# Decode attention with a cached K and V: 4 MB loads in one ring of five slots, another order of the last loads, wo per group, two K^T buffers, and a V lag of two steps

## The chip, the cores and the metric

The kernel runs on one core of a Trainium2 chip. The core has five engines with instruction streams of their own: TensorE (PE in the profile) for matrix products, VectorE (DVE), ScalarE (ACT), GpSimd (POOL) and SyncE (SP). Sixteen DMA engines move data between the chip's main memory and the core's on-chip memory of 128 partitions; SP and ScalarE start such transfers, each through a queue of its own. Engines wait for each other and for transfers through semaphores, and every engine works through its stream in order.

The metric is the device time of one execution in microseconds, as the median of several runs. One further execution is recorded by the hardware profiler.

## The reference

One token attends to a cache of 65,536 positions. There are 8 groups of K and V, and 2 query heads for each. The result is mixed with a small token MLP through a gate. Cut to what matters:

```python
Hq, Hkv, Sk, Dh = 16, 8, 65536, 256          # D = 448, everything bf16
q = (x @ wq).reshape(B, Sq, Hq, Dh).transpose(0, 2, 1, 3)     # Sq = 1
k = repeat(k_cache, 2, axis=1); v = repeat(v_cache, 2, axis=1)
scores = einsum("bhqd,bhkd->bhqk", q, k) * Dh ** -0.5
o = einsum("bhqk,bhkd->bhqd", softmax(scores), v)
a = o.transpose(0, 2, 1, 3).reshape(B, Sq, Hq * Dh) @ wo

h = layernorm(x)                              # the token MLP
u = gelu(einsum("bsd,sf->bdf", h, w1) + b1)   # F = 1792
b = (einsum("bdf,fs->bds", u, w2) + b2).transpose(0, 2, 1)

g = sigmoid((x * gate_w).sum(-1, keepdims=True))
return g * a + (1 - g) * b
```

K and V are 8 x 65,536 x 256 numbers of 2 bytes each: 268 MB for K and as much for V. Every byte is read once.

## The kernel before

**Tiling.** A chunk is `CH` = 2048 positions of one group: 16 tiles of 128 positions (`NT` = 16). A group has `NCPH` = 32 chunks, the whole kernel `NC` = 256. Position p*16+n of a chunk lies on partition p, so that a load reads one contiguous row of memory for each partition. A load (`DC` = 2) brings two chunks of K or of V: 2 MB, 16 KB on each partition. There are `NCD` = 128 loads of K and 128 of V.

**Loads.** SP issues all large transfers in one order: K load 0, wq in two parts, and then, for each cd, K load cd and V load cd-1 (L203 to L214). K has two buffers (`KB`), V three (`VB`). A K load waits until the transposes of the K load two before it are done (L187, `sem_tr`); a V load waits until the values of the V load three before it are done (L194, `sem_pv`). The last V load goes out in four pieces of 512 KB, each with a semaphore of its own (L199). wo, 3.5 MB, is one load after K load 3 (L213). ScalarE's queue brings the small rows at the start.

**TensorE's steps.** The loop at L327 runs `NC + LAG` steps. Step s does, in this order: the transposes of chunk s (L245: 32 of 128x128, into the four PSUM banks `kst`), the scores of chunk s-1 (L261: 32 products with two columns, from the transposed K in `ktT`), the denominators of chunk s-2 (L272: one product of a matrix of ones with the weights), and the values of chunk s-`LAG` (L287: 32 products with two columns). With `LAG` = 3 the values of a chunk come one step after its denominators. Step 1 also holds the Q projection (L339, L341), which needs wq. The MLP's output products (L308) lie in steps 6 to 19. At a group's end follows the projection with wo (L300, `project`).

**The other engines.** VectorE copies the banks 0 and 2 of each chunk from PSUM into `ktT` (L470), ScalarE the banks 1 and 3 (L533). `ktT` has three buffers (`KTB`); a copy into one waits for the scores that read it last. ScalarE turns scores into weights `pT` (L524, five buffers, `PTB`). VectorE computes the MLP's tiles in the loop's steps 3 to 18 (`b_partA`, `b_partB`), ScalarE their tanh (L518).

**The end.** After the last values VectorE sums the denominators (L450), inverts them (L454) and scales (L447); TensorE multiplies with wo (L300); VectorE adds the row (L461); SP stores it (L216).

Of the kernel before, what the change touches and what calls it, by code (L numbers as in the profile page):

```python
# [11 lines left out]
def bass_gated_mix__gqa_block_cached__mixer_token_mlp__decode_kernel(  # L12
# [25 lines left out]
    P = 128  # L38
# [6 lines left out]
    DC = 2  # L45
    KB = 2
    VB = 3
# [4 lines left out]
    KTB = 3  # L52
    PTB = 5
    LAG = 3
    assert T % (CH * DC) == 0 and NCD > max(KB, VB)

# [7 lines left out]
    PN = 8  # L64
    NPIECE = DC * NT // PN

# [16 lines left out]
    with ctx:  # L83
# [8 lines left out]

        kbuf = sb([P, KB, DC * NT, DH], bf16, "kbuf")
        vbuf = sb([P, VB, DC * NT, DH], bf16, "vbuf")
# [5 lines left out]
        wq_a = sb([P, WF, NQ], bf16, "wq_a")  # L100
        wq_b = sb([P, HALF], bf16, "wq_b")
        wo_sb = sb([P, HQ, 2, DM], bf16, "wo_sb")
# [7 lines left out]
        w1row_b = sb([1, F], bf16, "w1row_b")  # L110
        b1row_b = sb([1, F], bf16, "b1row_b")
        w2row_b = sb([1, F], bf16, "w2row_b")
# [5 lines left out]
        scr_row = sb([1, DM], f32, "scr_row")  # L118
        prod_b = sb([1, DM], bf16, "prod_b")
# [7 lines left out]
        wring = sb([P, NUR, DM], bf16, "wring")  # L127
        tring = sb([P, NUR, DM], bf16, "tring")
        gu = sb([P, NUR, DM], bf16, "gu")
        brow1 = sb([1, DM], bf16, "brow1")  # L130
        brow = sb([1, DM], bf16, "brow")
        run = sb([1, DM], f32, "run")
        out_b = sb([1, DM], bf16, "out_b")

# [3 lines left out]

        sem_k = [new_sem("semk%d" % i) for i in range(KB)]
        sem_v = [new_sem("semv%d" % i) for i in range(VB)]  # L140
        sem_vp = [new_sem("semvp%d" % i) for i in range(NPIECE)]
# [3 lines left out]
        sem_wo = new_sem("sem_wo")  # L145
# [30 lines left out]

        def cache_src(cache, cd, n0=0, n1=DC * NT):
            g, k = divmod(cd * DC, NCPH)
            src = cache[0, g, k * CH:(k + DC) * CH, :].rearrange("(p n) d -> p n d", p=P)
            return src[:, n0:n1, :].rearrange("p n d -> p (n d)")  # L180

        @block.sync
        def _(eng):
            def k_dma(cd):
                slot = cd % KB
                if cd >= KB:
                    eng.wait_ge(sem_tr, NB * (cd - KB + 1) * DC)  # L187
                eng.dma_start(kbuf[:, slot].rearrange("p n d -> p (n d)"), cache_src(A_k_cache, cd)
                              ).then_inc(sem_k[slot], 16)

            def v_dma(cd):
                slot = cd % VB
                if cd >= VB:
                    eng.wait_ge(sem_pv, (cd - VB + 1) * DC)  # L194
                if cd < NCD - 1:
                    eng.dma_start(vbuf[:, slot].rearrange("p n d -> p (n d)"), cache_src(A_v_cache, cd)
                                  ).then_inc(sem_v[slot], 16)
                    return
                for j in range(NPIECE):  # L199
                    eng.dma_start(vbuf[:, slot, j * PN:(j + 1) * PN, :].rearrange("p n d -> p (n d)"),  # L200
                                  cache_src(A_v_cache, cd, j * PN, (j + 1) * PN)).then_inc(sem_vp[j], 16)

            k_dma(0)  # L203
            eng.dma_start(wq_a[:, :, :].rearrange("p j n -> p (j n)"),
                          A_wq[0:WF * P, :].rearrange("(p j) n -> p (j n)", p=P)).then_inc(sem_wq, 16)
            eng.dma_start(wq_b[:, :], A_wq[WF * P:DM, :].rearrange("r (a n) -> (r a) n", a=2)
                          ).then_inc(sem_wq, 16)
            for cd in range(1, NCD + 1):
                if cd < NCD:
                    k_dma(cd)  # L210
                v_dma(cd - 1)
                if cd == KB + 1:
                    eng.dma_start(wo_sb[:, :, :, :].rearrange("p h j n -> p h (j n)"),  # L213
                                  A_wo.rearrange("(h p j) n -> p h (j n)", h=HQ, j=2)).then_inc(sem_wo, 16)  # L214
            eng.wait_ge(s_run, H + 1)
            eng.dma_start(out_row_ap, out_b[:, :]).then_inc(sem_out, 16)  # L216
            eng.wait_ge(sem_out, 16)
# [13 lines left out]
        def _(pe):  # L231
            one = ones_sq[0:1, 0:1]

            def transposes(c):
                cd, ck = divmod(c, DC)
                slot = cd % KB
                if ck == 0:
                    pe.wait_ge(sem_k[slot], 16 * (cd // KB + 1))
                for b in range(NB):
# [3 lines left out]
                    for j in range(8):  # L243
                        ntl, dh = divmod(j, 2)
                        ins = pe.transpose(kst[:, b, j * P:(j + 1) * P],  # L245
                                           kbuf[:, slot, ck * NT + 4 * b + ntl, dh * P:(dh + 1) * P],
# [28 lines left out]
            def values(c):  # L275
                g, k = divmod(c, NCPH)
                cd, cv = divmod(c, DC)
                slot = cd % VB
                if cd < NCD - 1 and cv == 0:
                    pe.wait_ge(sem_v[slot], 16 * (cd // VB + 1))  # L280
                for nt in range(NT):
                    n = cv * NT + nt
                    if cd == NCD - 1 and n % PN == 0:
                        pe.wait_ge(sem_vp[n // PN], 16)
                    for dj in range(2):
                        col = POC + dj * REP
                        ins = pe.matmul(acc[:, g % 2, col:col + REP],  # L287
                                        vbuf[:, slot, n, dj:DH:2],
# [5 lines left out]
            def project(g):  # L294
                pe.wait_ge(s_oTn, g + 1)
                if g == 0:
                    pe.wait_ge(sem_wo, 16)
                for hh in range(REP):
                    for dj in range(2):
                        ins = pe.matmul(acc[0:1, g % 2, PRC:PRC + DM],  # L300
                                        oTn[:, g % 2, dj * REP + hh:dj * REP + hh + 1],
                                        wo_sb[:, g * REP + hh, dj, :],
# [59 lines left out]
        def _(vec):  # L362
# [49 lines left out]
            def b_partA(kt):  # L412
                slot = kt % NUR
                U = uring[:, slot, :]; W = wring[:, slot, :]; Z = zring[:, slot, :]
                if kt >= NUR:
                    vec.wait_ge(s_tanh, kt - NUR + 1)
                    vec.drain()
# [148 lines left out]
```

The softmax here doesn't subtract the row's maximum and nothing guards it: scores larger than these inputs give would overflow.

## Time and profile before

| | |
|---|---|
| median of 4 runs | 1321.25 us (1320.61 to 1322.43) |
| the profiled execution, its own time | 1321.69 us |
| the profiled execution's span, first to last instruction | 1319.9 us |
| TensorE matmuls, busy | 1122.2 us, 85% of the span, 25054 matmuls |
| TensorE weight loads, busy | 1096.7 us, 83% |
| ScalarE, VectorE busy | 546.5 us (41%), 412.8 us (31%) |
| TensorE's clock granted, mean | 0.776 of full speed |
| read from main memory | 544.22 MB, 412 GB/s over the span |
| K loads, issue to landing, median | 12.6 us for 2048 KB |
| V loads, issue to landing, median | 17.3 us for 2048 KB |

The span is what the profile covers; the execution's own time has some 1.8 us more around it. "Busy" is the time in which an instruction of the engine runs; a matmul and the load of the next weights overlap. The weights' load belongs to each matmul here, because K, its transposed form and V are the stationary operands. "Granted clock" is the share of full speed at which the chip ran TensorE's array, which changes between half and full in the records. A wait in the profile names the instruction or transfer that released it; "issue" is time in which an engine waited for nothing that the profile shows. The DMA row of the page is the busy share of the 16 DMA engines.

### The profile page before, as it was taken

The numbers are of one execution on the slowest core, as the hardware profiler recorded it, in microseconds if no ns is written. First come the engines' busy times: TensorE is split into PE (matmuls) and PEld (weight loads), VectorE is DVE, ScalarE is ACT, GpSimd is POOL, SyncE is SP. The second block draws the span as 40 slices with busy tenths as digits, with TensorE's granted clock in tenths as the row PEclk, the third lists the DMA queues.
The fourth block names the chain that finished last, engine by engine and source line by source line (L and its number), as shares of the span: only waits on it lengthen the run. The fifth ranks groups of instructions, "written<-read, shape, count | busy, mean of one in ns | idle before, by whom it ended". The sixth has DMA issues, their size and how long they took to land.

```text
span 1319.9 us, 53238 instructions
## 1 busy us (share of the span) xinstructions
PE 1122.2 (85%) x25054; PEld 1096.7 (83%) x25054; DVE 412.8 (31%) x716; ACT 546.5 (41%) x786; POOL 0.9 (0%) x7
## 2 busy tenths in 40 slices
PE   6689888888899888988888898888878888888888
PEld 5688888888889888888888898888878888788887
DVE  3685223222222222222222222222223222232222
ACT  3344444444434344444433444344433443443343
POOL 0000000000000000000000000000000000000000
PEclk8778777878767787777767877777778777787877
DMA  9999999999999999999999999999999999999996
GB/s 396 422 425 423 419 424 410 425 420 418 426 398 426 425 417 423 423 422 413 411 421 400 424 417 423 423 419 421 414 419 426 411 426 414 412 428 420 422 423 274
DMA packets 39880, 547.64 MB, mean 415 GB/s; under 512 B 4200, under 2 KB 6251, under 8 KB 6894
## 3 DMA queue, kind: packets, MB, share of 16 engines
q1 hardware_dynamic: 39650, 544.23, 98.4%
q8 instruction: 197, 3.23, 1.0%
q14 instruction: 21, 0.17, 0.0%
q10 hardware_dynamic: 12, 0.01, 0.0%
HBM read 544.22 MB, written 0.00 MB: 412 GB/s over the span
## 4 chain that ended last, share of the span: by engine, by line
DMA 52%; PE 45%; issue 2%; DVE 0%; ACT 0%; ACTq 0%; DVEq 0%
DMA kbuf<-in_A_k_cache_dram 51%; PE kst L245 32%; PE acc L287 6%; PE sps L261 6%; DMA b_b<-in_B_b_dram 1%; PE acc L300 1%; PE acc L272 0%; PE sps L339 0%; PE acc L308 0%; ACT L511 0%; PE sps L341 0%; DVE out_b L461 0%; DVE ktT L470 0%; DVE stat L390 0%; ACTq L503 0%
## 5 line engine op out<-in xcount | busy, mean ns | idle before, releaser
L533 ACT ACTIVATE ktT<-kst 128x1024 bf16<-128x1024 bf16 x512 | 512.1, 1023 | 732.0 <-PE kst L245 731.8
L245 PE MATMUL kst<-ident,kbuf 128*128 128x128 bf16 x8192 | 698.1, 263 | 132.7 <-DMA kbuf<-in_A_k_cache_dram 122.5
L245 PEld LDWEIGHTS kst<-ident,kbuf 128*128 128x128 bf16 x8192 | 646.3, 121 | 149.1 <-DMA kbuf<-in_A_k_cache_dram 130.5
L470 DVE COPY ktT<-kst 128x1024 bf16<-128x1024 bf16 x512 | 352.8, 691 | 871.9 <-PE kst L245 858.0
L287 PE MATMUL acc<-pT,vbuf 128*128 128x2 bf16 x8192 | 247.4, 163 | 28.7 <-issue 28.7
L261 PE MATMUL sps<-qT,ktT 128*128 128x2 bf16 x8192 | 252.1, 164 | 19.1 <-issue 18.7
L261 PEld LDWEIGHTS sps<-qT,ktT 128*128 128x128 bf16 x8192 | 246.5, 99 | 20.9 <-issue 20.4
L287 PEld LDWEIGHTS acc<-pT,vbuf 128*128 128x128 bf16 x8192 | 228.7, 98 | 32.1 <-issue 32.1
L524 ACT ACTIVATE pT<-sps 128x32 bf16<-128x32 f32 x256 | 50.2, 196 | 21.1 <-PE sps L261 21.1
L272 PE MATMUL acc<-pT,ones_sq 128*128 128x32 bf16 x256 | 45.7, 179 | 1.0 <-ACT pT L524 0.5
L272 PEld LDWEIGHTS acc<-pT,ones_sq 128*128 128x128 bf16 x256 | 25.0, 98 | 0.0
L300 PE MATMUL acc<-wo_sb,oTn 128*1 128x448 bf16 x32 | 11.2, 484 | 0.9 <-DVE oTn L447 0.8
L323 PE MATMUL acc<-ones_sq,w1row_b 1*128 1x1 bf16 x14 | 0.5, 161 | 10.5 <-DMA b_b<-in_B_b_dram 10.5
L323 PEld LDWEIGHTS acc<-ones_sq,w1row_b 1*128 1x128 bf16 x14 | 0.4, 100 | 10.6 <-DMA b_b<-in_B_b_dram 10.6
L518 ACT ACTIVATE tring<-zring 128x448 bf16<-128x448 bf16 x14 | 8.1, 582 | 0.0
L300 PEld LDWEIGHTS acc<-wo_sb,oTn 128*1 128x1 bf16 x32 | 2.4, 94 | 4.4 <-issue 2.8
L428 DVE TENSOR_TENSOR zring<-uring,wring 128x448 bf16<-128x448 bf16 x14 | 5.5, 392 | 1.4 <-issue 0.4
L422 DVE TENSOR_TENSOR wring<-uring 128x448 bf16<-128x448 bf16 x14 | 5.5, 392 | 1.0
L424 DVE TENSOR_TENSOR zring<-wring,uring 128x448 bf16<-128x448 bf16 x14 | 5.5, 392 | 1.0
L441 DVE TENSOR_TENSOR gu<-wring,tring 128x448 bf16<-128x448 bf16 x14 | 5.5, 392 | 1.0
L308 PE MATMUL acc<-gu,w2p_b 128*1 128x448 bf16 x14 | 5.1, 363 | 0.0
L420 DVE TENSOR_SCALAR uring<-wring,params 128x448 bf16<-128x448 bf16 x14 | 4.7, 336 | 1.1
(68 smaller groups left out, 60.0 us busy)
## 6 DMA issues: line engine op xcount, KB each, us to landing
kbuf<-in_A_k_cache_dram SPq DMA_DIRECT2D x128, 2048.0 KB, 12.6
vbuf<-in_A_v_cache_dram SPq DMA_DIRECT2D x127, 2048.0 KB, 17.3
wo_sb<-in_A_wo_dram SPq DMA_DIRECT2D x1, 3584.0 KB, 23.5
wq_a<-in_A_wq_dram SPq DMA_DIRECT2D x1, 3072.0 KB, 14.7
vbuf<-in_A_v_cache_dram SPq DMA_DIRECT2D x4, 512.0 KB, 12.2
wq_b<-in_A_wq_dram SPq DMA_DIRECT2D x1, 512.0 KB, 15.4
xrow_b<-in_A_x_dram ACTq DMA_DIRECT2D x1, 0.9 KB
grow_b<-in_gate_w_dram ACTq DMA_DIRECT2D x1, 0.9 KB
```

What stands on the lines that cost most here:

```text
L245: ins = pe.transpose(kst[:, b, j * P:(j + 1) * P], kbuf[:, slot, ck * NT + 4 * b + ntl, dh * P:(dh + 1) * P], ident[:, :])
L261: ins = pe.matmul(sps[:, c % 2, 2 * nt:2 * nt + 2], ktT[:, slot, b, j * P:(j + 1) * P], qT[:, dh, REP * g:REP * g + REP], start=(dh == 0), ...
L272: pe.matmul(acc[:, g % 2, DENC:DENC + 2 * NT], ones_sq[:, :], pT[:, c % PTB, :], start=(k == 0), stop=(k == NCPH - 1))
L287: ins = pe.matmul(acc[:, g % 2, col:col + REP], vbuf[:, slot, n, dj:DH:2], pT[:, c % PTB, 2 * nt:2 * nt + 2], start=False, stop=(k == NCPH ...
L300: ins = pe.matmul(acc[0:1, g % 2, PRC:PRC + DM], oTn[:, g % 2, dj * REP + hh:dj * REP + hh + 1], wo_sb[:, g * REP + hh, dj, :], start=(hh ...
L422: vec.tensor_tensor(W, U, U, op=ALU.mult)
L424: vec.tensor_tensor(Z, W, U, op=ALU.mult)
L428: vec.tensor_tensor(Z, U, W, op=ALU.add)
L470: vec.tensor_copy(ktT[:, c % KTB, b, :], kst[:, b, :]).then_inc(sem_evd, 1)
L518: act.activation(tring[:, slot, :], zring[:, slot, :], AF.Tanh).then_inc(s_tanh, 1)
L524: act.activation(pT[:, c % PTB, :], sps[:, c % 2, 0:2 * NT], AF.Exp, scale=scale).then_inc(sem_exp, 1)
L533: act.activation(ktT[:, c % KTB, b, :], kst[:, b, :], AF.Copy).then_inc(sem_eva, 1)
```

## The change

- A load has four chunks: 4 MB, 32 KB on each partition (`DC` = 4), so that there are 64 loads of K and 64 of V.
- K and V share one ring of five slots (`NS`), used in the order of the loads: K0, V0, K1, V1, ... In this list the last K load changes places with the V load before it, so that the end reads K62, K63, V62, V63. Load i waits for the last reader of load i-5: transposes where that was K, values where it was V.
- wq and the MLP's row w2 lie in the ring's last slot at the start, w1 and b1 in the second K^T buffer. Load 4, the first in that slot, waits for the Q projection (`s_q`).
- The last V load goes out in pieces of 32, 16, 8 and 8 tiles (2 MB, 1 MB, 512 KB, 512 KB).
- wo comes in 8 loads of 448 KB, one for each group, into two buffers; load g waits for the projection of group g-2.
- `KTB` goes from 3 to 2, `PTB` from 5 to 4, `LAG` from 3 to 2.
- In the MLP the work row W is one buffer instead of three, tanh writes into its own input, a wait for tanh is dropped and two drains are added for each tile. Several rows of one partition share memory with others that are no longer needed.

```diff
-    DC = 2
-    KB = 2
-    VB = 3
+    DC = 4
+    NS = 5
...
-    KTB = 3
-    PTB = 5
-    LAG = 3
+    KTB = 2
+    PTB = 4
+    LAG = 2
...
+    loads = [(w, cd) for cd in range(NCD) for w in "kv"]
+    loads[-3], loads[-2] = loads[-2], loads[-3]
+    place = {ld: i for i, ld in enumerate(loads)}
...
+    pieces = [(0, 32), (32, 48), (48, 56), (56, 64)]
...
-        kbuf = sb([P, KB, DC * NT, DH], bf16, "kbuf")
-        vbuf = sb([P, VB, DC * NT, DH], bf16, "vbuf")
+        ring = sb([P, NS, DC * NT, DH], bf16, "ring")
...
+        early = ring[:, NS - 1, :, :].rearrange("p n d -> p (n d)")
+        wq_a = early[:, 0:WF * NQ].rearrange("p (j n) -> p j n", j=WF)
+        wq_b = early[:, WF * NQ:WF * NQ + HALF]
...
+        def slot_of(w, cd):
+            i = place[w, cd]
+            return i % NS, 16 * (i // NS + 1)
...
+            def load(i):
+                w, cd = loads[i]
+                slot = i % NS
+                if i == NS - 1:
+                    eng.wait_ge(s_q, 1)
+                if i >= NS:
+                    w0, cd0 = loads[i - NS]
+                    if w0 == "k":
+                        eng.wait_ge(sem_tr, NB * DC * (cd0 + 1))
+                    else:
+                        eng.wait_ge(sem_pv, DC * (cd0 + 1))
+                if i < len(loads) - 1:
+                    eng.dma_start(ring[:, slot].rearrange("p n d -> p (n d)"), cache_src(w, cd)
+                                  ).then_inc(sem_in[slot], 16)
                     return
...
+            def wo_dma(g):
+                if g >= 2:
+                    eng.wait_ge(s_proj, g - 1)
+                eng.dma_start(wo_sb[:, g % 2, :, :],
+                              A_wo[g * REP * DH:(g + 1) * REP * DH, :].rearrange("(h p j) n -> p h (j n)", h=REP, j=2)
+                              ).then_inc(sem_wo[g % 2], 16)
...
+            for i in range(1, len(loads)):
+                load(i)
+                g, r = divmod(i, 2 * NCPH // DC)
+                if r == NCPH // DC:
+                    wo_dma(g)
...
             def b_partA(kt):
                 slot = kt % NUR
-                U = uring[:, slot, :]; W = wring[:, slot, :]; Z = zring[:, slot, :]
-                if kt >= NUR:
-                    vec.wait_ge(s_tanh, kt - NUR + 1)
-                    vec.drain()
+                U = uring[:, slot, :]; W = wtmp[:, :]; Z = zring[:, slot, :]
+                vec.drain()
...
-                U = uring[:, slot, :]; W = wring[:, slot, :]; TT = tring[:, slot, :]
+                U = uring[:, slot, :]; W = wtmp[:, :]; TT = zring[:, slot, :]
                 vec.wait_ge(s_tanh, kt + 1)
+                vec.drain()
```

## The prediction

> **What bounds the kernel now.** I read the page's queue part first, then the waits, then the chain of waits, then the end of the timeline. First the DMA engines: share of 16 engines' span by queue, and busy tenths over 40 slices.
>
> ```profile
> DMA  9999999999999999999999999999999999999996
> ...
> q1 hardware_dynamic: 39650, 544.23, 98.4%
> q8 instruction: 197, 3.23, 1.0%
> ```
>
> The 16 engines are busy from slice 1 to 39, 98.4% of it with K, V and weights. Bytes cannot fall, so only their cost per byte, the head and the tail can move. Next who waits (total us, times, longest us):
>
> ```profile
> SPq L188 <- PE kst L245: 1165.5, 126, 17.3
> ...
> PE kst L245 <- DMA kbuf<-in_A_k_cache_dram: 122.5, 83, 8.4
> ...
> PE acc L287 <- issue: 28.7, 30, 2.2
> ...
> PE sps L261 <- issue: 18.7, 16, 2.4
> ...
> PE kst L245 <- issue: 9.8, 10, 2.7
> ```
>
> SP waits 1165.5 us for the transposes that free a K buffer, yet the engines stay full: when K load 127 is issued at 1289.73, load 126 has 2.8 us to go and a V load of about 5 us stands behind it, 7.8 us of queue. TensorE waits 122.5 us for K and 57.2 us for "issue". TensorE is thus second, by a small margin. How fast it can go, from the timeline (start, us, ...):
>
> ```profile
> 635.98 1.96 PE L245 MATMUL kst<-ident,kbuf 128*128 128x128 bf16 x32 [0.54 <-DMA kbuf<-in_A_k_cache_dram]
> ...
> 639.41 1.95 PE L245 MATMUL kst<-ident,kbuf 128*128 128x128 bf16 x32
> ...
> 645.76 3.59 PE L245 MATMUL kst<-ident,kbuf 128*128 128x128 bf16 x32 [2.80 <-DMA kbuf<-in_A_k_cache_dram]
> ...
> 650.93 3.57 PE L245 MATMUL kst<-ident,kbuf 128*128 128x128 bf16 x32
> ```
>
> A step (transposes, scores, denominators, values) is 639.41-635.98 = 3.43 us at full clock and 650.93-645.76 = 5.17 us at half clock; after a wait of 2.8 us the clock is half. DMA brings a step's 2 MB in 5.1 us. Last the end, from the chain of waits:
>
> ```profile
> 1289.73 12.51 DMA kbuf<-in_A_k_cache_dram
> ...
> 1302.29 2.80 PE kst L245 x32
> ...
> 1306.80 3.40 PE kst L245 x32
> 1310.20 0.78 PE sps L261 x32
> ...
> 1313.47 1.70 PE acc L287 x64
> ...
> 1315.91 1.67 PE acc L300 x4
> ...
> 1317.67 0.67 DVE out_b L461
> ```
>
> The last K lands at 1302.25, the last V piece at 1312.07 (its semaphore's record), so 4 MB took 9.8 us; TensorE ends its values at 1315.17. From last landing to the span's end: 1319.9-1312.1 = 7.8 us.
>
> **The change, part by part.** The trace keeps a record of every DMA packet (start, time, size; part 3 sums them). Median times: 4 bytes (semaphore) 0.009 us, 1792 bytes 0.074, 4 KB 0.159, 16 KB 0.611, 24 KB (wq_a) 0.912. These lie on one line: 0.009 us each plus 0.0367 us per KB. K and V now go as 16 KB rows, 8 per engine and load.
>
> *4 MB loads.* Rows of 32 KB would take 0.009+1.204 = 1.213 us against 2 x 0.611 = 1.222. Per engine 2072 K and V packets become 1048: 1024 x 0.009 = 9.2 us less. Of 262 DMAs on SP 142 remain; 120 semaphore packets per engine x 0.009 = 1.1 us less. Bounds: 1.1 us if the 9 ns is not per row, 10.3 if it is. I take 10.3; 24 KB, the nearest row, lies on the line. The 16 KB mean is 0.624, not 0.611, 26.6 us per engine in all; the long packets come in bursts on several engines at once, so I keep that per byte (if per packet, 13 us less: the lower end). The last landing moves to 1312.1-10.3 = 1301.8.
>
> [...]
>
> *Ring of five 32 KB slots.* K load c waits for the values of V load c-3, V load c for the transposes of K load c-2: 20 MB where 10 MB were buffered, so two to three loads of 9.9 us are queued. SP is in order: behind each wait stands the next load alone, which is wanted two loads later. DMA cannot run dry in steady state. The head: load 4 holds wq and waits for the Q projection (20.6 us in the trace, some 5 us later now, because K load 0 is twice as long and the small ACT loads, landed by 13.1 now, take turns with packets twice as long); loads 0 to 3 and wq keep DMA busy to 1.7+4x9.9+8.6 = 50 us, which covers it. If not covered it would cost its lateness once.
>
> *wo per group.* Same 2048 packets of 1792 bytes, 7 more DMAs of about 0.4 us on SP, which waits most of the time; each is asked for half a group before its use and its wait on an old projection is long past. Nothing.
>
> *Two K^T buffers, PTB 4, shared work rows, two more drains per mixer tile.* The eviction of chunk c needs the scores of c-2, which TensorE issued before these transposes: no wait. The drains (28, at 0.03 us and 0.04 us of issue, as L453's in the chain) lie on VectorE in steps 3 to 18, behind DMA's 20 us queue. Nothing; uncovered, under 2 us.
>
> *V lag of two and the last K load one place ahead: the tail.* The order ends K62, K63, V62, V63. TensorE is in order: step 250 has the first values of V62 behind its transposes. K62 and K63 are there long before, but V62 lands only one load (9.8 us) before the end, and TensorE stands for some 8 us until then, so the clock falls. Then come: values 248, 0.83; steps 251 to 254, one or two of them at half clock, 5.2+4.3+2x3.43 = 16.3; the transposes of 255, 1.8; three scores/values pairs, one without scores, 4.2 (one V less than now, by the lag); the close 1319.9-1315.2 = 4.7; half a us of fetch stalls. Sum 28.3, less 9.8: 18.5 us from last landing to the end, now 7.8. Bounds 17 (one slow step) to 21 (three) and 24 with fetch stalls. This part costs 10.7 us.
>
> Sum: -10.3 + 10.7 = +0.4, span 1320.3. The profiled execution's span is 1319.9, its own time 1321.69; the median 1321.25 is 1.35 over the span. Forecast 1321.7.
>
> **Rivals.** *Slower: instruction fetch.* Queue q8 brings TensorE's instructions: 25054 matmuls, as many loads and 395 semaphore waits are 197 x 256, so 16 KB is a block. The "issue" waits begin at block borders, 127 matmuls apart. A block's packet starts 3.4 us (median; 2.1 to 4.8 for the middle 80%) after TensorE enters the block before it, takes 1.05, and TensorE goes on 1.35 us after: 5.8 us a block at best. Near the end, with the queues empty, the packet starts after 0.35 to 0.7, so some 3 us are queueing, five packets of 16 KB. If five packets stay ahead, these become 6 us and a block 8.8: 25+197x8.8+8 = 1767 us. It decides from (1320-33)/197 = 6.5 us a block, 0.7 over now, and each 0.1 beyond costs 20 us. Against: the fetch at 53.59 waited 4.3 us behind wo's packets of 0.074 us, so the wait looks like bytes or time, not a count; then only the packet in service grows, +0.3 us, and nothing shows. For: fetches start just as a data packet ends.
>
> [...]
>
> *Slower: no gain per row* (a 32 KB row is split, or reads slower): 1312.1-1.1+18.5 = 1329.5, so 1331. Against it 24 KB on the line.
>
> *Faster:* the long packets come per packet; half of 26.6 goes, 13 us: 1309. Bursts across engines speak against it. A part of it, or no half-clock steps in the tail, gives 1314 to 1318.
>
> **How the numbers follow.** Forecast 0.47, own range 1318 to 1326; fetch 0.28, from 1322 upward, half of it beyond 1360; no row gain 0.12; faster 0.13. Range 1312 to 1365, leaving 0.05 below and 0.14 above. A measurement here tells 0.2%, 2.6 us, from no change. Faster: 0.13 and 0.04 of the forecast = 0.17. Within: 0.34 of the forecast and 0.04 of fetch = 0.38. Slower: 0.09, 0.24 and 0.12 = 0.45. Slower has more in all, but spread over two cases; the single likeliest is no change.
>
> **What would show it.** Packets of 32 KB at 1.21 us; semaphore packets halved; last landing near 1302; TensorE idle some 8 us before values 248, then about 28 us to the end. "Issue" waits near 60 us mean no fetch case; several hundred mean it. K waits vanishing with DMA under 400 GB/s would mean that TensorE became the bound. Wrong would be an early last landing with a short tail, or an order of values that does not stop step 250.

## The result and the profile after

| | before | after |
|---|---|---|
| median of all runs | 1321.02 us (54 runs, 1319.41 to 1323.18) | 1322.9 us (34 runs, 1320.68 to 1331.32) |
| ratio, 95% interval | | 1.0022 (1.0014 to 1.003) |
| profiled execution, own time / span | 1321.69 / 1319.9 us | 1321.53 / 1319.7 us |
| last data packet ends | 1311.6 us | 1303.3 us |
| last values end | 1315.15 us | 1315.0 us |

The forecast was 1321.7 us. The change costs 0.2% in the median, and the executions have one new trait, which was not forecast: they scatter over 10.6 us, where they lay within 3.8 us. The lowest 13 of the 34 lie within 1320.7 to 1321.7, the highest 7 above 1328. The profiled execution, at 1321.53 us, is one of the shorter ones, and what is read from it holds for those.

A row, which is what one packet carries (before, 32640 packets of 16384 bytes in the records; after, 16256 of 32768), is a run of consecutive positions on one partition: 32 positions or 16 KB before (position p*32+n of a load lies on partition p, not p*16+n as the description of the kernel has it), 64 positions or 32 KB after.

The page of the kernel after, DMA engines' busy tenths, packets, and queues (packets, MB, share):

```profile
DMA  9999999999999999999999999999999999999992
...
DMA packets 21559, 547.62 MB, mean 415 GB/s; under 512 B 2264, under 2 KB 4315, under 8 KB 4702
...
q1 hardware_dynamic: 21330, 544.22, 97.0%
q8 instruction: 197, 3.23, 1.0%
```

The data's share of the span falls from 98.4% to 97.0%, and slice 40 from 6 to 2. The DMA engines end earlier, but the span does not. Packets of 32 KB took 1.213 us in the median, to the third digit the predicted time of one packet. The waits of TensorE after (total us, times, longest):

```profile
PE kst L259 <- DMA ring<-in_A_k_cache_dram: 47.4, 31, 3.2
PE acc L303 <- issue: 46.0, 45, 2.5
PE sps L275 <- issue: 37.6, 30, 2.4
PE kst L259 <- issue: 29.0, 24, 2.8
...
PE acc L303 <- DMA ring<-in_A_v_cache_dram: 5.5, 1, 5.5
...
PE kst L259 <- ACT ktT L547: 1.4, 1, 1.4
PE kst L259 <- DVE ktT L484: 1.4, 2, 0.8
...
PE sps L275 <- ACT ktT L547: 1.2, 1, 1.2
...
PE sps L275 <- DVE ktT L484: 0.8, 1, 0.8
```

The wait for K fell from 122.5 to 47.4 us, and what came in its place is the wait for instructions: with 2.0 and 1.3 us of smaller lines, 115.9 us against 57.8. Together the two kinds are 168.8 us with the V wait, against 180.3. The last four lines, 4.8 us, are waits for the copies of K^T, which the matmuls before did not have. The end, from TensorE's timeline (start, us, instruction, idle before it):

```profile
1287.12 0.19 PE L286 MATMUL acc<-pT,ones_sq 128*128 128x32 bf16 x1
1292.80 1.02 PE L303 MATMUL acc<-pT,ring 128*128 128x2 bf16 x32 [5.49 <-DMA ring<-in_A_v_cache_dram]
1293.68 3.57 PE L259 MATMUL kst<-ident,ring 128*128 128x128 bf16 x32
...
1298.73 1.95 PE L259 MATMUL kst<-ident,ring 128*128 128x128 bf16 x32
```

TensorE stood 5.49 us in step 250 for V62, its next transposes ran at half clock (3.57 us for 32), the ones after at full clock (1.95 us). The chain of waits has the same end:

```profile
1261.90 30.86 DMA ring<-in_A_v_cache_dram
...
1292.80 1.02 PE acc L303 x32
1293.82 3.44 PE kst L259 x32
...
1314.19 0.84 PE acc L303 x32
...
1317.53 0.67 DVE out_b L475
```

So the last 22 us after V62's landing are TensorE's own work without a wait, and the span ends 16.4 us after the last landing.

### The profile page after: what moved, and what is told of

The parts are those of the page before. It is cut to its first block, busy times and chain, and to the rows that moved or that the text cites. A ratio compares the mean times of both kernels' runs of the same rounds, so it can differ in the third digit from the quotient of the medians.

```text
span 1319.7 us, 53069 instructions
## 1 busy us (share of the span) xinstructions
PE 1126.6 (85%) x25054; PEld 1100.9 (83%) x25054; DVE 413.8 (31%) x716; ACT 549.9 (42%) x786; POOL 0.9 (0%) x7
## 4 chain that ended last, share of the span: by engine, by line
PE 49%; DMA 43%; issue 6%; DVE 1%; ACT 1%; DVEq 0%; ACTq 0%
DMA ring<-in_A_k_cache_dram 40%; PE kst L259 29%; PE acc L303 9%; PE sps L275 9%; DMA ring<-in_A_v_cache_dram 2%; DMA b_b<-in_B_b_dram 1%; PE acc L315 0%; PE acc L286 0%; ACT ktT L547 0%; DVE ktT L484 0%; PE sps L354 0%; ACT zring L532 0%; PE acc L323 0%; DVE zring L437 0%; DVE zring L441 0%
## 5 line engine op out<-in xcount | busy, mean ns | idle before, releaser
L259 PE MATMUL kst<-ident,ring 128*128 128x128 bf16 x8192 | 705.4, 264 | 79.9 <-DMA ring<-in_A_k_cache_dram 47.4
L259 PEld LDWEIGHTS kst<-ident,ring 128*128 128x128 bf16 x8192 | 651.4, 122 | 94.5 <-DMA ring<-in_A_k_cache_dram 52.7
L303 PE MATMUL acc<-pT,ring 128*128 128x2 bf16 x8192 | 250.9, 164 | 51.8 <-issue 46.0
L303 PEld LDWEIGHTS acc<-pT,ring 128*128 128x128 bf16 x8192 | 231.0, 99 | 57.5 <-issue 51.9
L532 ACT ACTIVATE zring<-zring 128x448 bf16<-128x448 bf16 x14 | 8.1, 577 | 2.7 <-DVE zring L443 2.7
L437 DVE TENSOR_TENSOR zring<-wtmp,uring 128x448 bf16<-128x448 bf16 x14 | 5.5, 392 | 1.5 <-issue 0.5
L435 DVE TENSOR_TENSOR wtmp<-uring 128x448 bf16<-128x448 bf16 x14 | 5.5, 392 | 1.2 <-issue 0.2
L441 DVE TENSOR_TENSOR zring<-uring,wtmp 128x448 bf16<-128x448 bf16 x14 | 5.5, 392 | 1.0
L455 DVE TENSOR_TENSOR gu<-wtmp,zring 128x448 bf16<-128x448 bf16 x14 | 5.5, 392 | 1.0
```

The source lines that it names most:

```text
L259: ins = pe.transpose(kst[:, b, j * P:(j + 1) * P], ring[:, slot, ck * NT + 4 * b + ntl, dh * P:(dh + 1) * P], ident[:, :])
L303: ins = pe.matmul(acc[:, g % 2, col:col + REP], ring[:, slot, n, dj:DH:2], pT[:, c % PTB, 2 * nt:2 * nt + 2], start=False, stop=(k == NCPH ...
L435: vec.tensor_tensor(W, U, U, op=ALU.mult)
L437: vec.tensor_tensor(Z, W, U, op=ALU.mult)
L441: vec.tensor_tensor(Z, U, W, op=ALU.add)
L532: act.activation(zring[:, slot, :], zring[:, slot, :], AF.Tanh).then_inc(s_tanh, 1)
```

## The experiments

All were timed against the kernel before. "Landing" is the end of the last data packet in the profiled execution; the two kinds of waits are TensorE's totals there.

| kernel | median, runs, range (us) | ratio (95%) | landing | issue / K and V waits | clock |
|---|---|---|---|---|---|
| before | 1321.02 (54) | 1 | 1311.6 | 57.8 / 122.5 | 0.776 |
| after | 1322.9 (34, 1320.68-1331.32) | 1.0022 (1.0014-1.003) | 1303.3 | 115.9 / 52.9 | 0.766 |
| e1, order not swapped | 1322.74 (12, 1318.47-1329.5) | 1.002 (1.0006-1.0034) | 1302.5 | 141.0 / 21.8 | 0.764 |
| e2, 16 KB rows | 1331.5 (5, 1329.2-1331.55) | 1.0079 (1.0067-1.0091) | 1311.6 | 77.7 / 111.2 | 0.773 |
| e3, V lag of 4 | 1326.04 (9, 1320.91-1330.6) | 1.0035 (1.002-1.0051) | 1306.4 | 166.9 / 7.9 | 0.767 |
| e4, e1 and last K load in pieces | 1324.26 (8, 1318.89-1332.58) | 1.0025 (1.0004-1.0046) | 1304.0 | 158.4 / 2.9 | 0.744 |
| f1, e4 with 16 KB rows | 1326.97 (5, 1326.52-1329.42) | 1.005 (1.0038-1.0062) | 1311.7 | 89 / 109.8 | 0.779 |
| g1, e4 with half the value products | 1306.78 (4, 1306.45-1307.1) | 0.9891 (0.9876-0.9905) | 1297.1 | 53.8 / 257.2 | 0.804 |
| g2, e4 with half-width transposes | 1320.57 (10, 1316.44-1325.67) | 0.9995 (0.998-1.0009) | 1303.7 | 284.5 / 14.9 | 0.513 |
| g3, g2 with 16 KB rows | 1325.69 (5, 1325.42-1326.45) | 1.0033 (1.0021-1.0046) | 1311.8 | 104 / 205.9 | 0.511 |
| h1, last 8 values at the very end | 1323.21 (12, 1317.8-1333.87) | 1.0022 (1.0-1.0043) | 1302.9 | 148 / 23.9 | 0.774 |
| i2, e4 with half of the values wide | 1316.32 (5, 1315.3-1319.57) | 0.9965 (0.9952-0.9977) | 1299.6 | 55 / 88.5 | 0.888 |
| i1, all values wide but the last group's | 1313.47 (5, 1311.63-1316.68) | 0.9936 (0.9922-0.9949) | 1297.3 | 11.5 / 89.8 | 0.955 |
| j1, wide to the last four chunks | 1309.99 (5, 1309.91-1310.13) | 0.9919 (0.9906-0.9933) | 1296.8 | 0.9 / 74.9 | 0.972 |

Some expectations below give waits of a fetch after a block's border. Where these were counted at a fixed 127 matmuls a block they drift, since the border's place against that count moves by some 28 matmuls in the kernels with the ring; the second table of the next section counts each border from the stops beside it, and replaces such figures.

### e1: the last loads in plain order

```diff
-    loads[-3], loads[-2] = loads[-2], loads[-3]
```

> The changed kernel with the last loads in plain order, K62, V62, K63, V63. Tail theory: V62 then lands two loads before the end and no longer stops step 250; K63 lands 9.8 us before the end, behind it stand steps 252 to 255 (one or two at half clock: 5.2+4.3+2x3.4 = 16.3 us less the 0.8 of no extra values), 4.2 us of last scores and values and 4.7 us of close: 9.8 us before the end plus 25 us is 15 us at most and 13 at best after the last landing, where the changed kernel has 16.4 to 18.5. The last landing stays near 1303. Time 1317 to 1319, 2 to 5 us under the changed kernel. Rival, that TensorE's instruction fetch sets the time: the order of two loads moves nothing, 1321 to 1324, and the last landing does not matter. Rival, that the exchange helps because K63 is there early: 3 to 5 us slower.

The profiled execution took 1318.47 us, as the tail's theory says, and the lowest of 12 runs are 2.2 us below the lowest after. The median is no better: 1322.74. So, read from the lowest runs alone, the swapped order costs some 2 us in those executions in which TensorE keeps up with the loads, and most executions are set by something else. The waits point to it: 141.0 us for instructions, 21.8 for K.

### e2: the same ring with rows of 16 KB

```diff
-                    eng.dma_start(ring[:, slot].rearrange("p n d -> p (n d)"), cache_src(w, cd)
-                                  ).then_inc(sem_in[slot], 16)
+                    for n0, n1 in ((0, 32), (32, 64)):
+                        eng.dma_start(ring[:, slot, n0:n1, :].rearrange("p n d -> p (n d)"),
+                                      cache_src(w, cd, n0, n1)).then_inc(sem_in[slot], 16)
```

> The changed kernel with each whole load sent as two transfers of 2 MB into the same slot, so rows of 16 KB again and twice the semaphore packets; buffers, order and tail stay. Row theory (0.009 us for each packet): 1016 more packets of data and some 127 more of semaphores per engine, 10.3 us; last landing 1313 to 1314, time 1331 to 1333, the same tail. Rival, that the cost is per byte: 1322 to 1324. Rival, that fetch behind 32 KB packets sets the time of the changed kernel: rows of 16 KB bring the issue waits back from 115 us to some 60 and the time down, below 1322. On the wait of a fetch before its packet starts (5.1 us median with 32 KB rows, 3.4 before): a count of packets in front of it gives 3.4 again, a fixed number of bytes gives 5.

The landing went 8.3 us back, and the time 8.6 us up, with the runs within 2.4 us. This is the price of the row together with that of its semaphore packets, of which e2 has 127 more per engine; the expected 1331 to 1333 us was met, with a landing 1.4 us earlier than the expected 1313 to 1314. TensorE's waits in e2:

```profile
PE kst L260 <- DMA ring<-in_A_k_cache_dram: 103.1, 56, 4.8
PE acc L304 <- issue: 41.2, 36, 2.3
PE sps L276 <- issue: 23.1, 21, 1.9
```

With the shorter rows TensorE waits for K again (103.1 us) and less for instructions. The scatter went with it: in all these runs it is wide only where TensorE waits little for data (52.9 us and less in the table).

### e3: a V lag of four

```diff
-    PTB = 4
-    LAG = 2
+    PTB = 6
+    LAG = 4
```

> The changed kernel, exchange kept, with LAG 4 and PTB 6: the first values of V62 then stand in step 252, not 250. Tail theory: when V62 lands 9.8 us before the end only steps 253 to 255 with transposes stand behind it, so two steps of transposes, scores and so on leave the tail and two steps of values come in: about 0.8+5.2+2x3.4+1.6+0.9+2x0.8 = 17 us in place of 23 behind V62's landing. Time 1315 to 1317, 5 to 7 us under the changed kernel. Rival, that fetch or the rate of TensorE sets the time: no change. Rival, that the later release of V buffers (two steps, some 10 us of a queue of 20) lets DMA run dry: last landing later than 1305 and time above 1322.

A miss: 1326.04 instead of 1315 to 1317. With the longer lag TensorE no longer stands for V62, but K waits are 7.9 us in all and issue waits 166.9: TensorE was the later of the two for nearly the whole span. The values of each chunk come two steps later, so slots come free later; the DMA engines stood idle for 9.0 us before the last 30 us, against 3.9 after. The landing of 1306.4 us and the time fit the third case of the expectation, that the late release lets DMA run dry; the issue waits fit the second, and this run does not part the two.

### e4: plain order and the last K load in four pieces

```diff
-    loads[-3], loads[-2] = loads[-2], loads[-3]
...
+    kpieces = [(0, 16), (16, 32), (32, 48), (48, 64)]
...
+                if i == len(loads) - 2:
+                    for (n0, n1), sem in zip(kpieces, sem_kp):
+                        eng.dma_start(ring[:, slot, n0:n1, :].rearrange("p n d -> p (n d)"),
+                                      cache_src(w, cd, n0, n1)).then_inc(sem, 16)
+                    return
...
-                if ck == 0:
+                if cd == NCD - 1:
+                    pe.wait_ge(sem_kp[ck], 16)
+                elif ck == 0:
```

> Plain order of the last loads, and K63 sent in four pieces of 1 MB, each with a semaphore of its own, so that chunk 252 can start 7.3 us earlier. Tail theory: TensorE has K63's first piece 17 us before the end and ends its transposes about when the last V lands; tail 6 to 9 us after the last landing near 1303.5, time 1311 to 1314, 9 to 12 us under the changed kernel and 7 to 10 under the kernel before. Also the spread of the runs (1320.7 to 1331.3 for the changed kernel) should shrink to some 3 us, because a long run of steps at half clock no longer stands behind the last landing. Rival, that TensorE is the bound at the end anyway: 1318 or more.

The largest miss: 1324.26 us in the median instead of 1311 to 1314, and a scatter of 13.7 us instead of 3. It removes what was thought to make the tail, and the profiled execution, one of the longest, took 1331.66 us. Its waits, and a stretch of its timeline:

```profile
PE acc L311 <- issue: 74.0, 59, 3.2
PE sps L283 <- issue: 52.1, 45, 2.9
PE kst L267 <- issue: 29.3, 27, 2.6
...
PE kst L267 <- DMA ring<-in_A_k_cache_dram: 2.9, 1, 2.9
```

```profile
1270.68 0.59 PE L311 MATMUL acc<-pT,ring 128*128 128x2 bf16 x18
1273.09 0.52 PE L311 MATMUL acc<-pT,ring 128*128 128x2 bf16 x14 [1.82 <-issue]
1273.47 3.44 PE L267 MATMUL kst<-ident,ring 128*128 128x128 bf16 x32
```

In the timeline the values of one chunk are cut after 18 matmuls, TensorE stands 1.82 us with K and V long in place, and the transposes behind it run at half clock (3.44 us for 32). TensorE waited once for K in the whole kernel and ended its values 21 us after the last landing. This gave the new theory: TensorE, held by its instruction fetch, is the bound in many executions. The next runs test it.

### f1: e4 with rows of 16 KB

```diff
-            return i % NS, 16 * (i // NS + 1)
+            return i % NS, 32 * (i // NS + 1)
...
+                    for n0, n1 in ((0, 32), (32, 64)):
+                        eng.dma_start(ring[:, slot, n0:n1, :].rearrange("p n d -> p (n d)"),
+                                      cache_src(w, cd, n0, n1)).then_inc(sem_in[slot], 16)
```

> The kernel of e4 (plain order, K63 in four pieces) with rows of 16 KB as in e2. In e4 TensorE never waited for K or V (2.9 us), had 158 us of issue waits, and ended its values 21 us after the last landing. Theory now: behind 32 KB rows TensorE is the bound, by its instruction fetch; with 16 KB rows it keeps ahead of DMA (e2: K waits 103 us, issue 78 us), and only then does the earlier K63 shorten the tail. Last landing 1312, tail 6 to 9, time 1319 to 1323, runs within 3 us of each other; 9 to 12 us under e2's 1331.5. Rival, that the pieces don't work whatever the rows: 1330, as e2.

1326.97 us, above the 1319 to 1323 expected: 4.5 us under e2, so plain order and K pieces do pay where DMA is the bound. The runs lie within 3 us. What is missing went to issue waits and half clock in the last steps.

### g1: half of the value products left out

```diff
+                    if nt % 2:
+                        continue
```

> The kernel of e4 without the values of every second tile: half of the value products, 32 of a step's 202 TensorE instructions and 0.4 us of its time, are left out; loads and order stay. If TensorE is the bound (fetch or array), its blocks per step fall by 16%: K waits come back above 60 us, last landing near 1303, time 1308 to 1313. If the last loads' order or the last landing's variation set the time of e4: 1320 to 1330 as e4.

1306.78 us, 17.5 under e4, by doing less on TensorE only. TensorE's waits:

```profile
PE kst L267 <- DMA ring<-in_A_k_cache_dram: 257.2, 62, 6.2
PE sps L283 <- issue: 23.7, 21, 2.6
```

One wait for nearly each of the 64 K loads: DMA is the bound again, and the four runs lie within 0.7 us. TensorE was the bound in e4. The landing itself came 6.9 us earlier than in e4.

### g2: the same instructions with half the streamed columns

```diff
-                        ins = pe.transpose(kst[:, b, j * P:(j + 1) * P],
-                                           ring[:, slot, ck * NT + 4 * b + ntl, dh * P:(dh + 1) * P],
-                                           ident[:, :])
+                        w = P if c < 4 else P // 2
+                        ins = pe.transpose(kst[:, b, j * P:j * P + w],
+                                           ring[0:w, slot, ck * NT + 4 * b + ntl, dh * P:(dh + 1) * P],
+                                           ident[0:w, 0:w])
```

> The kernel of e4 with transposes of 64 of the 128 positions of a tile from chunk 4 on (the rest of the bank keeps old data): the same number of TensorE instructions, half of the columns streamed, so 0.9 us less array time in a step at full clock and 1.7 us less at half clock. If fetch is the bound, the blocks still take about 6.2 us each, issue waits rise to 250 us or more and the time stays within 10 us of e4, 1316 to 1328. If the array and its clock are the bound, the time falls to DMA's, 1308 to 1313, with issue waits as in e4.

A transpose here takes in 64 of a tile's 128 positions, so it streams half of the columns, from half of the partitions (`64*128 64x64` in the profile, where e4 has `128*128 128x128`; 32 of them take 1.89 us at half clock, where e4's take 3.44); the scores of the other positions are left out. This is to tell apart what of TensorE is the bound: its arithmetic or its instructions. The page (busy us and share; the clock in tenths), and then the waits:

```profile
PE 991.2 (75%) x25054; PEld 931.4 (71%) x25054; DVE 413.7 (31%) x716; ACT 540.0 (41%) x786; POOL 0.9 (0%) x7
...
PEclk9555555555555555555555555555555555555555
```

```profile
PE acc L312 <- issue: 109.7, 63, 2.8
PE sps L284 <- issue: 93.8, 58, 2.6
PE kst L268 <- issue: 77.6, 57, 2.6
PE kst L268 <- DMA ring<-in_A_k_cache_dram: 14.9, 8, 3.4
```

TensorE's busy time fell by 156 us against e4's 1147.5, of which 126 us became issue waits, 12 us waits for K and 14 us a shorter span. The two profiled executions flatter this step, e4's being among its longest and g2's among its shortest: between the medians the gain is 3.7 us. With the arithmetic shortened the time still did not fall below 1316.44 in any run, and 284.5 us of issue waits stand against 14.9 for K: here the fetch sets the pace. Its packets start 6.56 us apart in the mean (a quarter below 6.18, a quarter above 7.03).

### g3: g2 with rows of 16 KB

The edit is that of f1.

> The kernel of g2 (from chunk 4 on, half of the positions of each tile are left out of the transposes) with rows of 16 KB. In g2 fetch alone set the pace: blocks 6.56 us apart in the mean, many at 6.1 and many at 7.1, which differ by one 32 KB packet of 1.2 us. If a fetch's start is held up by the packet in service, 16 KB rows give 6.2 to 6.3 us a block, issue waits fall from 284 us to some 240, K waits come back to 30 us or more, and the last landing near 1312 sets the time: 1318 to 1324. If rows don't matter to the fetch: the mean interval of 6.56 and issue waits of 280 us stay.

1325.69 us, 1.7 above the 1318 to 1324 expected; issue waits fell far more than to the expected 240 us. The waits:

```profile
PE kst L269 <- DMA ring<-in_A_k_cache_dram: 205.9, 63, 5.7
PE acc L313 <- issue: 58.4, 47, 2.1
```

With nothing changed but the row, issue waits fell from 284.5 to 104 us and K waits rose to 205.9. The longer row itself slows the fetch (a block that ends in a stop takes about 6.1 us here and 6.66 in g2), and it also lets data come 8.1 us earlier; between the two rows the later of the two engines changes.

### h1: the last eight chunks' values after all other steps

```diff
-    PTB = 4
+    PTB = 12
+    LATE = 8
...
-                if 0 <= s - LAG < NC:
+                if 0 <= s - LAG < NC - LATE:
                     values(s - LAG)
...
+            for c in range(NC - LATE, NC):
+                values(c)
```

> The changed kernel, exchange kept, with the values of the last 8 chunks after all other steps (PTB 12), so that V62 stops no transposes. Tail theory alone: K63 lands 19.5 us before the end, its steps without values take 3 to 4.3 us each, 8 values of 0.83 us follow, 4.7 us of close: 8 to 10 us after the last landing near 1303, time 1312 to 1315. TensorE as the bound: it comes to the end late by what it lost in the middle, so 1316 to 1326 with a spread of some 8 us over the runs, as the changed kernel, and under it by at most the wait for V62, 5.5 us.

Median 1323.21, lowest 1317.8, highest 1333.87: like e1 and e4, no gain in the median from a better tail, though the lowest run lies 2.9 us under the lowest after.

### i1, i2 and j1: fewer and wider value products

The whole result is computed. A value product now holds the weights' two columns as stationary operand and streams 256 columns of V, so that 16 products do what 32 did; at a group's end two small products turn the sum into the form that the projection needs. i2 does so for 8 of 16 tiles.

```diff
+                    if g < H - 1 and nt % 16 >= 16 - WIDE:
+                        ins = pe.matmul(acc[0:REP, g % 2, PRC:PRC + DH],
+                                        pT[:, c % PTB, 2 * nt:2 * nt + 2],
+                                        ring[:, slot, n, :],
+                                        start=False, stop=(k == NCPH - 1 and nt == NT - 1),
+                                        skip_group_check=True)
+                        continue
...
+            def fold(g):
+                pe.wait_ge(s_osb, g + 1)
+                for dj in range(2):
+                    col = POC + dj * REP
+                    ins = pe.matmul(acc[:, g % 2, col:col + REP], osb[0:REP, g % 2, dj:DH:2],
+                                    ident[0:REP, 0:REP], start=False, stop=True,
+                                    skip_group_check=True)
+                ins.then_inc(s_fold, 1)
```

> The kernel of e4, whole computation kept, with another form of the values in groups 0 to 6: the weights are the stationary operand (128x2) and V streams through, 16 products of 256 columns in place of 32 of 2; a group's end has two small products more that turn the result. A step then has 170 TensorE instructions instead of 202. If the instruction fetch (6.56 us a block in g2, where nothing else limits TensorE) is what bounds TensorE, a step's share falls from 5.18 to 4.36 us, under DMA's 4.97, and e4's early K63 works: K waits above 60 us, time 1309 to 1314, runs within 3 us. Array theory: more columns are streamed, 4.35 us a step at full clock and 7.7 at half, so it is slower than e4, above 1330.

> As i1_wide16 with 8 of the 16 tiles of a chunk in the new form: 186 instructions a step, 4.77 us by fetch at 6.56 us a block, 3.9 us of array time at full clock and 6.5 at half. Fetch theory: just under DMA's 4.97 us, K waits of 20 to 60 us, time 1310 to 1318, more spread than i1. Array theory: between e4 and i1, above 1326.

1313.47 and 1316.32 us: the gain against e4's 1324.26 grows with the number of tiles. i1's issue waits are 11.5 us, and its mean clock is 0.955; the last group keeps the old form, and there the clock falls to 7 tenths. j1 takes the new form up to the last four chunks:

```diff
-                    if g < H - 1 and nt % 16 >= 16 - WIDE:
+                    if c < NC - 4 and nt % 16 >= 16 - WIDE:
...
+            fold(H - 1)
             project(H - 1)
```

> i1_wide16 with the new form of the values in the last group too, except in its last four chunks, and the turn of the result at its end as well; whole computation kept. In i1 the last group, in the old form, fell behind again: its last 33 us hold 2.9 us of issue waits and five steps at half clock, and values end 12.8 us after the last landing. Fetch theory: with 170 instructions a step TensorE keeps full clock and stays with DMA to the end; last landing 1297 to 1299, tail 7 to 10 us (one of it the added turn), span 1305 to 1309, time 1307 to 1311. Rival, that i1's tail is only the order of the last loads: 1312 to 1315, as i1.

1309.99 us, 0.8% under before, all five runs within 0.22 us. Its page and a step of its timeline:

```profile
PE 1210.6 (93%) x21038; PEld 1037.5 (79%) x21038; DVE 415.9 (32%) x724; ACT 531.2 (41%) x786; POOL 0.9 (0%) x7
...
PEclk9999999989998989999999898998999998999899
...
q8 instruction: 165, 2.70, 0.8%
```

```profile
648.65 1.96 PE L271 MATMUL kst<-ident,ring 128*128 128x128 bf16 x32
650.45 0.94 PE L287 MATMUL sps<-qT,ktT 128*128 128x2 bf16 x32
651.25 0.18 PE L298 MATMUL acc<-pT,ones_sq 128*128 128x32 bf16 x1
651.36 1.91 PE L314 MATMUL acc<-ring,pT 128*2 128x256 bf16 x16
653.20 1.96 PE L271 MATMUL kst<-ident,ring 128*128 128x128 bf16 x32
```

TensorE is busier (93%) and yet faster: a step takes 653.20-648.65 = 4.55 us at full clock here, the mean clock is 0.972, 165 blocks are fetched instead of 197, and issue waits are 0.9 us. What remains is 74.9 us of waits for K. How much of it is the fewer blocks and how much the clock, these three runs do not separate; g1, whose clock was only 0.804, had the same landing with as few blocks.

## Why the prediction was right, and where its steps failed

**The size was right by two terms that were each a little too large, and partly by luck.** Predicted were -10.3 for the last landing and +10.7 for the tail. Measured, both by the last data packet: 1303.3-1311.6 = -8.3, and (1319.7-1303.3)-(1319.9-1311.6) = +8.1. The span is 0.2 us shorter, where +0.4 was forecast. This is one of the shorter executions; the median is 1.9 us longer than before by the scatter, for which the sum had no term. At the start DMA moved 402 GB/s over the first 30 us against 393 before, so the buffers did not run dry, and no view shows a wait for wo. For the two K^T buffers the prediction had "no wait"; TensorE's five waits for their copies came to 4.8 us, none of them in the last 22 us.

**The landing: near in size, by errors that cancel.** The packet records give, up to the last landing, how long an engine carried packets and how long it did not (mean over 16 engines, us), and by how much the packets of K and V exceeded their usual time of 0.611 or 1.213 us, summed for each engine:

| | landing | carrying | idle, last 30 us | idle, earlier | excess |
|---|---|---|---|---|---|
| before | 1311.6 | 1303.1 | 2.5 | 4.3 | 26.7 |
| e2, ring with 16 KB rows | 1311.6 | 1296.5 | 9.7 | 3.8 | 20.0 |
| after | 1303.3 | 1288.0 | 9.7 | 3.9 | 17.5 |
| e4 | 1304.0 | 1294.4 | 2.2 | 5.7 | 24.0 |
| j1 | 1296.8 | 1281.8 | 9.4 | 3.8 | 12.7 |

The rows and their semaphore packets alone, e2 to after, take 8.5 us off the carrying, where the working had 10.3. Its price of 0.009 us for a packet was too high: in the records 99% of the packets of K and V before, and 98% after, start 3 to 4 ns before another packet ends, which I take for the one ahead on the same engine, so that a packet spared gave 5 to 6 ns, some 6 us for 1016 rows and 127 semaphore packets. The other 2.5 us are a smaller excess.

The ring with the same rows and all else of the change, before to e2, takes another 6.6 us off the carrying, for which the sum had no term. It is the excess again, 26.7 to 20.0 us: 639 packets took over 1.2 times their usual time before, 431 in e2. And this is given back at the end: for 17.8 of the last 30 us before the last landing at most 9 of the 16 engines still work, against 4.0 us before. The records do not name the engines; the groups are read from the 16 semaphore packets of each load, one from each engine: eight engines had done all their packets by 1286.2, the others ended from 1301.3 to 1303.3, and already at 600 us the semaphore packets come in two groups (around 600.7 and 605.5). So the -8.3 is -8.5 and -6.6 with +7.2 of idle engines at the end and -0.4 of idle earlier, and two terms that the sum did not have happened to cancel.

That the two to three loads in the queue are what lets one group run ahead was not tested. In e4, where TensorE is late and slots come free late, the groups end together (2.2 us), but the carrying is 6.4 us longer than after, so the landing is no earlier.

The faster rival held that the excess comes per packet and halves with longer rows. It fell by 9.2 us, but by 6.7 of them with the rows unchanged. Where only the row changed it fell by 2.5 us (e2 to after) and 2.4 (g3 to g2), and rose by 4.5 (f1 to e4). So the rival's mechanism is not borne out, and the prediction's "per byte" is the nearer of the two.

**The tail: right mechanism, a little smaller.** 16.4 us against 18.5, below the bound of 17. TensorE stopped where predicted, for 5.5 us and not 8, and a single step ran at half clock. Steps 251 to 254 took 15.3 us for 16.3, there was no fetch stall for the 0.5 put there, and V62 landed 10.5 us before the last load and not 9.8.

**The step that failed is the fetch.** It held that a block takes "5.8 us a block at best", that the case "decides from (1320-33)/197 = 6.5 us a block, 0.7 over now", and that with longer packets "only the packet in service grows, +0.3 us, and nothing shows". The base was right for rows of 16 KB, the growth was too small. The time from a block's border to the start of the next fetch's packet, and the length of blocks that end in such a stop:

| kernel, row | wait, median | wait, 90% below | block that ends in a stop, median |
|---|---|---|---|
| before, 16 KB | 3.40 | 4.15 | 5.88 |
| e2, 16 KB | 3.56 | 4.15 | 5.92 |
| f1, 16 KB | 3.53 | 4.08 | 5.86 |
| after, 32 KB | 3.73 | 4.75 | 6.32 |
| e4, 32 KB | 3.96 | 4.76 | 6.52 |
| g2, 32 KB | 4.15 | 4.74 | 6.66 |
| g3, 16 KB | 3.6 | 4.1 | 6.1 |

With rows of 16 KB a block that ends in a stop takes 5.86 to 5.92 us, which is the working's 5.8, and 6.1 in g3. With rows of 32 KB it takes 6.32 us after, 6.52 in e4 and 6.66 in g2: 0.4 to 0.8 us more, where 0.3 was put, so that little or nothing was left of the 0.7 in hand. Where "nothing shows" was forecast, the issue waits doubled, from 57.8 to 115.9 us; by the prediction's own signs, near 60 us against several hundred, that is between its two cases.

The depth of the ring changes little (before, e2 and f1 agree within 0.16 us), so the fetch does not stand behind the queued loads, as the larger part of the fetch rival had it. Over all blocks the row adds 0.2 to 0.4 us to the median wait, and 0.6 to 0.7, half a long packet, at the 90% mark (where the prediction had 4.8 us for the kernel before, and 4.15 is found). In g2, where nearly every block stops TensorE, the wait is 4.18 us in the mean, the packet 1.06 and the resumption 1.4: 6.64 us, and 6.65 is measured. Why a block takes longer there than after, with the same rows, is not known.

In steps it is plainer. A step has 97 of a block's 127 matmuls: 6.65 x 97/127 = 5.08 us if the fetch paces every block as in g2, 6.32 x 97/127 = 4.83 by the stops after, and 5.88 x 97/127 = 4.49 by those before. DMA after the change needs 1288.0/256 = 5.03 us a step, and before it needed 1303.1/256 = 5.09. The change thus brought the two together from both sides, and which of them comes last varies between executions: so I read the scatter, which no run proves. The clock is a second reading beside it: a step at half clock, 5.17 us in the prediction's rows, is longer than DMA's 5.03, and in e4 the transposes behind a stop of 1.82 us for the fetch ran at half clock (3.44 us for 32, above). g2 shows that the fetch alone can hold TensorE back; no run prices the clock alone. It is shown that kernels with slack on TensorE (e2, f1, g1, g3, i1, i2, j1: within 0.2 to 5.1 us) scatter less than those without (after, e1, e3, e4, g2, h1: 9.2 to 16 us), though over fewer runs each. None of the longer executions of the changed kernel itself was profiled; e4's at 1331.66 us is the nearest. A step of j1 has 81 matmuls, 6.65 x 81/127 = 4.24 us by the fetch and 4.55 by TensorE's own work, against 1281.8/256 = 5.01 by DMA.

**What stays open.** Why eight engines run faster than the others. What makes some packets take longer than usual, and why there are fewer of them with the ring: in the three of the fourteen profiles in which the groups end together the excess is 26.7 us (before), 24.0 (e4) and 21.8 (e3), in the others 12.7 to 20.0, but this is seen side by side, not tested. Holding the groups together therefore need not bring the 7 us. With fewer fetched blocks data land earlier still (1297 in g1, i1 and j1); from after to j1 the carrying falls by 6.2 us (1288.0 to 1281.8) and the excess by 4.8, while 32 fetch packets of 1.06 us are only 2.1 us of mean.

## What to carry to other kernels

When a kernel is bound by loads, ask what the second engine's pace is if it never waits for data, under the changed kernel's own conditions (here with the long rows, as in g2), and not from the profile before with a small allowance; a gain on the first can be no larger than that gap. The number of instructions matters beside the bytes: halving the value products by making each wider took 14 us from e4 (1324.26 to 1309.99), more than any order of the loads, though how much of it is the higher clock was not separated. And a mean over DMA engines hides the slowest of them: look at how many are still busy in the last 20 us (after, at most 9 of 16 worked for 17.8 of the last 30 us, at a share of 97.0% over the span).

## What the runs showed of the hardware that was not expected

- Packets overlapped a little: before, 99% of those of K and V start 3 to 4 ns before another packet ends, and after 98%. If that is the one ahead on the same engine, as I take it, a packet cost its engine 3 to 4 ns less than its recorded time (0.611 us for 16 KB, 1.213 for 32 KB, 0.009 for a semaphore).
- In the changed kernel the sixteen DMA engines fell into two groups of eight with different pace, by the semaphore packets of the loads: one group was done by 1286.2 us, the other 15 to 17 us later (1301.3 to 1303.3). In e4, with the same 20 MB of ring but a later TensorE, the mean idle time in the last 30 us was only 2.2 us, as against 9.7.
- A deeper queue of loads hardly delayed the instruction fetch: the wait's median was 3.40 us with 10 MB of buffers (before) and 3.56 with 20 MB (e2, the same rows). The length of the row did: 3.53 us in f1 with 16 KB, 3.96 in e4 with 32 KB.
- In these four runs the granted clock went with how much the matmuls streamed more than with how busy TensorE was. g2, busy 75% of the span with transposes of 64 columns (from 64 of the 128 partitions) and products of two columns, was granted 0.513 of full speed; g1, busy 74% with transposes of 128 columns, 0.804; e4, busy 86%, 0.744; j1, busy 93% with values of 256 columns, 0.972.
